# One attention-plus-gate kernel, and a new order for its opening

## The chip, the cores and the metric

The kernel runs on one core of a Trainium2 chip. The time is device microseconds of that core; lower is better. The kernel before was timed in three runs: 668.15 us in the median, 666.78 to 668.41. A further execution was profiled.

## What is computed

The inputs are q, k and v (4 batches, 8 heads, 768 positions, 64 columns each) and two weight matrices of 512 x 2048 and 2048 x 512. Cut to what matters, the reference is:

```
k_sum = max of k over blocks of 32 positions;  v_sum = mean of v over the same blocks
scores_l = q k^T / 8, kept only where |i - j| < 16;  scores_s = q k_sum^T / 8 + log(32)
a = softmax over both together
x = a [v; v_sum], heads side by side, as (3072, 512)
h = x w_in;  g = h where h >= 1, 0 where h <= -1, (h + 1)^2 / 4 between
out = g w_out
```

All inputs and outputs are float32.

## The kernel before

The 3072 rows of x are worked on in eight chunks of 384, two to a batch. For each chunk, four pairs of heads p go through attention; then 16 blocks f of the hidden width go through the two feed-forward matmuls. A float32 product is made of three matmuls in a faster 32-bit format: each operand is split into a high half (the rounded value) and a rest, and high x high, high x rest and rest x high are added. The weights have to be split once, which is part of the first chunk. They come as 16 pieces of 128 x 2 x 512 ("weight pairs", i): pair 0 holds the blocks 0 and 1 of w_in, pair i block i - 1 of w_out and block i + 1 of w_in. A piece arrives as 64-bit words, and its float32 values are put together from the two 32-bit halves of a word on the chip.

Each piece of work is a *step*, written as a letter and its indices, and these are the ones the prediction speaks of:

- `r`, `k`, `q`, `y`, `v`: loads of keys, key windows, queries, values and value windows for a chunk c and a pair of heads p; `w`: the load of a weight pair (lines 104 to 108); `m`: the load of the mask and the unit matrix.
- `K`, `R`, `C`: a window of keys is copied together, the maximum over blocks taken (line 222), and copied behind the window (225). `Y`, `Z`, `V`, `W`: the sum of values over blocks (229), its turn on TensorE (233), its mean (237), and that spread over six blocks (241).
- `S`, `M`, `E`, `D`, `N`: scores (253), mask and maximum (261, 266), exponentials (271), reciprocal of the denominator (276, 277), normalisation (281).
- `T`, `P`: turn of the probabilities on TensorE (286) and their copy out of PSUM (291 on VectorE, 293 on ScalarE). `A`, `X`, `L`: probabilities times values (300), high half of x (307 or 309) and its rest (314).
- `a`, `b`, `c`, `d`, `e`, for a weight pair: first scaling (line 118 on GpSimd, 120 on ScalarE), second scaling (125), six joins on VectorE (133, 136, 141), high half (146 on GpSimd, 148 on ScalarE) and rest (154).
- `F`: the first feed-forward matmul of chunk c, block f, quarter k (324, three matmuls); `G`, `H`, `I`, `J`, `O`: the gate (330; square at 334 on VectorE or 336 on ScalarE; 339; high half 344; rest 349); `B`: the second feed-forward matmul (358, nine matmuls); `U`, `o`: copy and store of a result.

So F030 is chunk 0, block 3, quarter 0, and c24 the fifth join of weight pair 2.

What happens in the opening (the first chunk, the preparation of all weights, the attention of the second chunk, the loads for the third) is written out by hand in the string `OPENING`: 540 steps in the order in which they enter the program. Every engine takes its own instructions from that list, strictly in that order, so a step that waits holds up everything behind it on its engine. The loads stand in SyncE's queue in the same way. Six small tables say on which engine some steps run. Behind the opening, a loop gives the order on TensorE for the remaining seven chunks; there the other engines' order is set by the scheduler.

Buffers also set the order: two for h and the gate's t, two for the gate's rests, three ("w") shared by converted weights, loaded keys and values and results, six in PSUM for everything but h.

Of the kernel before, what the change touches and what calls it, by code (L numbers as in the profile page):

```python
# [40 lines left out]
OPENING = """
r01 q01 K01 R01 C01 r00 R00 K00 C00 m S01 M01 q00 r03 S00 q03 y01 r02 R03 E010 E011 K03 C03 y00 M00 E001 w0 D01 S03
E000 N010 N011 K02 R02 a0 C02 T010 T011 Y01 Y00 P011 D00 M03 P010 b0 c00 c01 v01 Z01 V01 W01 c02 N000 N001 q02 Z00
E030 E031 c03 c04 v00 A01 V00 D03 T000 X01 P000 w1 c05 T001 P001 W00 N031 S02 T031 b1 L01 d0 N030 M02 y03 y02 v03
k10 Y03 a1 c10 c11 q10 T030 c12 c13 e0 E020 E021 D02 C10 Z03 A00 V03 P031 X00 P030 c14 w2 v02 L00 c15 W03 N021 N020
d1 S10 A03 X03 a2 F000 b2 Y02 v10 w3 T020 F010 Z02 V02 W02 w4 T021 k11 P020 P021 M10 c20 c21 E100 e1 q11 F011 F001
A02 L03 c22 X02 L02 Z10 F002 F003 a3 c23 c24 E101 D10 b3 N100 N101 a4 w5 G00 F012 V10 H00 c25 c30 c31 d2 I00 b4 T100
F013 G01 c32 c33 c34 T101 F020 F021 J00 H01 c40 c35 C11 P101 F022 P100 e2 d3 I01 J01 S11 F023 c42 c41 F030 F031 F032
c44 c43 c45 O00 G02 H02 B00 I02 b5 e3 a5 F040 O01 M11 w6 w7 d4 b6 F033 w8 w9 F041 c50 c51 J02 c52 G03 a6 c53 c54 W10
B01 F042 H03 O02 e4 I03 A10 c55 c60 F043 c61 a7 b7 J03 F050 G04 H04 B02 E110 E111 c62 c63 c64 d5 e5 F051 I04 O03 c65  # L50
c70 v11 q20 wa c71 c72 c73 c74 c75 J04 F060 a9 F052 d6 O04 e6 b9 c90 a8 c91 F061 B03 F062 c92 c93 c94 d7 F053 F063
G05 G06 k20 H05 I05 H06 B04 q13 b8 Z11 wc wb I06 c95 F070 k13 q12 wf wd v12 k12 we e7 c80 c82 c84 J05 J06 V11 F080
c81 c83 c85 F071 F081 r20 aa d9 O05 F072 Z12 F082 F073 O06 ba X10 L10 G07 H07 F083 G08 bb H08 e9 B05 I07 ac ca0 ca1
bc J07 ca2 I08 ca4 ca3 cc0 ca5 d8 D11 e8 F0a0 B06 F0a1 F090 F0a2 J08 cc1 O07 C13 O08 da F091 F0a3 F092 cc2 cc4 cc3
ea G0a ab V12 H0a cc5 cb0 I0a B07 F093 dc ad G09 H09 ec cb2 J0a B08 cb4 bd S13 F0b0 I09 F0d0 J09 cb1 cb3 cb5 F0b1
F0d1 F0b2 M13 F0d2 W12 O09 N110 C12 F0b3 cd1 cd0 cd2 be db eb O0a ae G0b H0b B09 I0b T110 cd4 cd3 ce0 ce2 J0b cd5
E130 P110 ce1 ce4 ce3 ce5 F0c0 F0d3 G0d O0b N111 B0a dd ed W11 F0c1 E131 H0d I0d D13 T111 F0c2 B0b F0c3 F0e0 P111
S12 de G0c H0c I0c bf J0c A11 X11 af ee F0e1 M12 L11 cf0 cf1 cf2 R20 E120 E121 J0d F0f0 F0e2 F0f1 N130 O0c O0d D12
cf4 cf3 cf5 B0c F0f2 F0e3 F0f3 B0d G0e H0e G0f N121 Z13 I0e H0f v13 I0f df C20 N120 T121 P121 T120 N131 F100 P120
F110 J0e V13 T131 J0f A12 T130 F111 ef O0e B0e P131 O0f W13 P130 X12 L12 A13 X13 L13 F112 F101 B0f F102 F113 F103  # L60
U01 U02 U00 o01 o02 o00
"""
# [8 lines left out]


@with_exitstack
def fused_kernel(ctx: ExitStack, tc: tile.TileContext, q2, kT, kwin, vT, vwin, w_in, w_out, mask, ident, out):
# [38 lines left out]
    def convert_top(i):  # L113


        _, top = raws[i]
        if f"{i:x}" in A_POOL:
            nc.gpsimd.tensor_scalar_mul(out=top.bitcast(F32), in0=top.bitcast(F32), scalar1=2.0 ** -112)  # L118
# [24 lines left out]
    def convert_high(i):  # L143
        halves[i] = room(i, "halves", [P, 2, 2 * DM], F32R)
        if i in HI_POOL:
            nc.gpsimd.tensor_copy(out=halves[i][:, 0], in_=converting[i].bitcast(F32))
# [141 lines left out]
    def turned(c, p, j):  # L288
        pts[c, p, j] = att.tile([P, T], F32, tag=f"pt{j}", name=f"pt{c}_{p}_{j}", bufs=1)
        if f"{c}{p}{j}" in P_DVE:  # L290
            nc.vector.tensor_copy(out=pts[c, p, j][:KA], in_=t_pss[c, p, j][:KA, :T])
# [40 lines left out]
    def gate_square(c, f):  # L332
        if f"{c}{f:x}" in H_DVE:
            nc.vector.tensor_tensor(out=ts[c, f], in0=ts[c, f], in1=ts[c, f], op=ALU.mult)  # L334
        else:
            nc.scalar.square(out=ts[c, f], in_=ts[c, f])  # L336
# [169 lines left out]
```

## Time and profile before

| | |
|---|---|
| median of 3 runs | 668.15 us |
| the profiled execution | 667.64 us, of which 665.9 us from first to last instruction (the span) |
| granted TensorE clock, mean | 0.991 |
| TensorE busy | 631.3 us (95%) |
| VectorE / ScalarE / GpSimd busy | 255.5 / 365.8 / 282.6 us |
| read from memory / written | 56.51 / 6.29 MB |

The first thing to see is that the shares of the whole span hide the opening: VectorE is busy for 38% of the span and GpSimd for 42%, but in the first fifth of it both are nearly full, and in the rest they have little to do beside a TensorE that never stops. In the profile's rows PE is TensorE, PEld its weight loads, DVE VectorE, ACT ScalarE, POOL GpSimd, SP SyncE; L118 is line 118 of the kernel; a row of a group gives the output and inputs, the shape, the count, then the busy time, the mean time of one in ns, and the idle time in front of them with the engine that ended it. A row of a timeline gives start, length, engine, line and, in brackets, the idle time ahead and what ended it.

### The profile page before, as it was taken

The page shows a single profiled execution, that of the slowest core. Times are in us where ns is not written, and L with a number is a line of the kernel's source. Part 1 is how long each engine was busy: PE and PEld are TensorE (multiplying, and loading weights), DVE is VectorE, ACT ScalarE, POOL GpSimd, SP SyncE. Part 2 cuts the span into 40 slices and gives each one's busy share as a digit, 9 for nine tenths or more (in the row PEclk, how much of TensorE's full clock was granted, in tenths as well). Part 3 has the DMA queues.
Part 4 walks back from the last instruction along what each step waited for, and adds up shares of the span by engine and source line. Part 5 has one row for each costly group of instructions (what it writes and reads, how often), then busy time and mean ns, then how long its engine had stood idle before and what let it go on. Part 6 is the DMA issues. An engine that isn't in the chain of part 4 may idle for free.

```text
span 665.9 us, 11707 instructions
## 1 busy us (share of the span) xinstructions
PE 631.3 (95%) x4448; PEld 555.1 (83%) x4448; DVE 255.5 (38%) x497; ACT 365.8 (55%) x940; POOL 282.6 (42%) x305
## 2 busy tenths in 40 slices
PE   3588899989999999999999999999999999999997
PEld 2467788768988888898888989888888998889996
DVE  5778898662222322144222422235222222211111
ACT  4678877355455554555555555465554645544332
POOL 3899997543333323333333333334323323322221
PEclk9889999999999999999999999999999999999999
DMA  9999941171113311062121401144210100000001
GB/s 308 290 320 306 313 143 53 50 252 36 53 53 105 95 53 30 25 203 91 53 53 54 143 7 50 53 151 143 53 52 22 69 19 19 1 34 14 1 1 47
DMA packets 49767, 63.55 MB, mean 95 GB/s; under 512 B 24880, under 2 KB 33328, under 8 KB 49712
## 3 DMA queue, kind: packets, MB, share of 16 engines
q1 hardware_dynamic: 49712, 62.81, 31.7%
q8 instruction: 35, 0.57, 0.4%
q14 instruction: 20, 0.16, 0.1%
HBM read 56.51 MB, written 6.29 MB: 94 GB/s over the span
## 4 chain that ended last, share of the span: by engine, by line
PE 83%; POOL 8%; DVE 3%; DMA 2%; issue 2%; ACT 1%; SPq 0%; POOLq 0%; ACTq 0%
PE acc L358 37%; PE h L324 37%; PE o_ps L300 3%; POOL halves L154 3%; POOL raw L118 3%; PE s_ps L253 3%; PE t_ps L286 3%; DMA raw<-in_w_in 1%; POOL glo L349 1%; DMA mask_sb<-in_mask 1%; POOL e L281 1%; DVE c L133 0%; DVE c L136 0%; DVE t L334 0%; PE vs_ps L233 0%
## 5 line engine op out<-in xcount | busy, mean ns | idle before, releaser
L324 PE MATMUL h<-xhi,halves 128*128 128x384 f32 x1024 | 289.9, 342 | 7.3 <-POOL halves L154 3.3
L358 PE MATMUL acc<-halves,ghi 128*128 128x512 f32 x768 | 239.6, 393 | 0.0
L349 POOL TENSOR_TENSOR glo<-t,ghi 128x384 fp32r<-128x384 f32 x128 | 129.8, 1015 | 204.4 <-ACT ghi L344 204.1
L324 PEld LDWEIGHTS h<-xhi,halves 128*128 128x128 f32 x1024 | 188.5, 189 | 18.3 <-POOL halves L154 5.8
L339 DVE SCALAR_TENSOR_TENSOR t<-h,t 128x384 f32<-128x384 f32 x128 | 71.1, 557 | 269.6 <-ACT t L336 256.1
L324 PE MATMUL h<-xlo,halves 128*128 128x384 f32 x512 | 173.1, 338 | 0.2 <-DVE xlo L314 0.2
L358 PEld LDWEIGHTS acc<-halves,ghi 128*128 128x128 f32 x768 | 144.4, 188 | 27.2
L358 PE MATMUL acc<-halves,glo 128*128 128x512 f32 x384 | 153.8, 400 | 2.6 <-POOL glo L349 2.6
L330 ACT ACTIVATE t<-h,ones_half 128x384 f32<-128x384 f32 x128 | 73.9, 578 | 125.7 <-PE h L324 120.5
L271 ACT ACTIVATE e<-e,den 128x120 f32<-128x120 f32 x192 | 73.3, 383 | 56.0 <-DVE den L266 55.9
L344 ACT CAST ghi<-t 128x384 fp32r<-128x384 f32 x128 | 65.3, 513 | 64.4 <-DVE t L339 64.4
L324 PEld LDWEIGHTS h<-xlo,halves 128*128 128x128 f32 x512 | 96.7, 189 | 4.5 <-DVE xlo L314 0.5
L358 PEld LDWEIGHTS acc<-halves,glo 128*128 128x128 f32 x384 | 72.2, 188 | 15.8 <-POOL glo L349 3.5
L281 POOL TENSOR_TENSOR e<-e,den 128x360 f32<-128x360 f32 x64 | 49.6, 796 | 54.3 <-ACT t L330 40.3
L336 ACT ACTIVATE t<-t 128x384 f32<-128x384 f32 x126 | 66.0, 525 | 3.6
L225 POOL COPY k<-ks 128x144 f32<-128x144 f32 x30 | 9.2, 308 | 70.4 <-DMA k<-in_kwin 50.9
L154 POOL TENSOR_TENSOR halves<-w,halves 128x1024 fp32r<-128x1024 f32 x16 | 38.5, 2411 | 0.9 <-ACT halves L148 0.4
L241 POOL COPY v<-v 24x640 f32<-24x640 f32 x30 | 21.5, 718 | 36.5 <-issue 32.4
L300 PEld LDWEIGHTS o_ps<-pt,v 120*64 120x64 f32 x720 | 24.7, 143 | 14.6 <-ACT ghi L344 7.4
L271 ACT ACTIVATION_READ_ACCUMULATOR e<-e,den 128x1 f32 x192 | 36.0, 187 | 0.0
L314 DVE TENSOR_TENSOR xlo<-o_ps,xhi 128x384 fp32r<-128x384 f32 x32 | 17.8, 555 | 43.1 <-ACT xhi L309 43.1
L300 PE MATMUL o_ps<-pt,v 120*64 120x64 f32 x720 | 29.1, 232 | 4.2 <-POOL v L241 2.1
(56 smaller groups left out, 437.2 us busy)
## 6 DMA issues: line engine op xcount, KB each, us to landing
k<-in_kwin SPq DMA_DIRECT2D x28, 360.0 KB, 4.2
v<-in_vwin SPq DMA_DIRECT2D x30, 288.0 KB, 3.1
raw<-in_w_in SPq DMA_DIRECT2D x16, 512.0 KB, 10.4
raw<-in_w_out SPq DMA_DIRECT2D x16, 512.0 KB, 9.9
out<-o SPq DMA_DIRECT2D x24, 256.0 KB, 2.1
q<-in_q SPq DMA_DIRECT2D x56, 96.0 KB, 4.2
kraw<-in_kT SPq DMA_DIRECT2D x13, 384.0 KB, 4.2
vraw<-in_vT SPq DMA_DIRECT2D x13, 384.0 KB, 3.7
```

The lines of the kernel that those rows point to most:

```text
L154: nc.gpsimd.tensor_tensor(out=lo, in0=converting[i].bitcast(F32), in1=hi.bitcast(F32), op=ALU.subtract)
L241: nc.gpsimd.tensor_copy(out=mean[:, 1:], in_=mean[:, :1].broadcast_to([NSUM, NB - 1, P]))
L271: nc.scalar.activation(out=e[:, t, :], in_=e[:, t, :], func=AF.Exp, bias=nm[:, t:t + 1], scale=1.0, accum_out=den[:, t:t + 1])
L281: nc.gpsimd.tensor_tensor(out=e, in0=e, in1=den.unsqueeze(2).broadcast_to([P, NT, KA]), op=ALU.mult)
L300: nc.tensor.matmul(o_pss[c, p][j * D:(j + 1) * D, cols], v_ts[c, p][:KA, blk, j * D:(j + 1) * D], pts[c, p, j][:KA, cols], start=True, sto ...
L324: nc.tensor.matmul(hs[c, f][:, :T], weight["win", f][w][:, k * P:(k + 1) * P], x, start=(k == 0 and n == 0), stop=(k == NK - 1 and n == 2))
L330: nc.scalar.activation(out=ts[c, f], in_=hs[c, f][:, :T], func=AF.Relu, bias=ones_half, scale=0.5)
L336: nc.scalar.square(out=ts[c, f], in_=ts[c, f])
L339: nc.vector.scalar_tensor_tensor(out=ts[c, f], in0=hs[c, f][:, :T], scalar=1.0, in1=ts[c, f], op0=ALU.max, op1=ALU.min)
L344: nc.scalar.copy(out=hi, in_=ts[c, f])
L349: nc.gpsimd.tensor_tensor(out=lo, in0=ts[c, f], in1=hi.bitcast(F32), op=ALU.subtract)
L358: nc.tensor.matmul(acc[c][i], a[:, rows], weight["wout", f][w], start=(f == 0 and n == 0), stop=(f == NF - 1 and n == 2))
```

## The change

The list `OPENING` holds the same 540 steps in another order, and the tables name other engines for some of them. No step is added or taken away, and nothing behind the opening changes in the source.

```diff
 OPENING = """
-r01 q01 K01 R01 C01 r00 R00 K00 C00 m S01 M01 q00 r03 S00 q03 y01 r02 R03 E010 E011 K03 C03 y00 M00 E001 w0 D01 S03
...
+r01 r00 K01 R00 R01 q01 K00 C01 C00 m q00 S01 M01 E010 E011 S00 r02 R02 M00 E000 E001 q02 r03 D01 K02 C02 K03 N010
...
-K_COPY = "gggg"
-H_DVE = "0c 0f".split()
-P_DVE = "111 121 130 131".split()
-X_DVE = "12 13".split()
-A_POOL = "0 1 2 3 4 5 9 a d".split()
-HI_POOL = [1, 5, 8, 13]
+K_COPY = "gvgg"
+H_DVE = "".split()
+P_DVE = "130".split()
+X_DVE = "".split()
+A_POOL = "".split()
+HI_POOL = [0, 1, 2, 3, 4, 5, 7, 9, 10, 11, 12, 15]
```

In words: all 16 first scalings run on ScalarE (nine ran on GpSimd). Twelve high halves of weights run on GpSimd (four did). All gate squares are on ScalarE (two were on VectorE), as are all copies of x (two were on VectorE) and all copies of turned probabilities but one (four were on VectorE). The key window of heads p = 1, the pair with which the opening starts, is copied on VectorE (all four were on GpSimd).

The first place is GpSimd's queue around the first two weight pairs. In these rows `e_...` are probabilities, `raw_...` the words of a weight pair, `w_...` its joined values, `halves_...` its two halves, `first_91` value windows, `k_0_...` a window of keys. Before:

```order
L281 TENSOR_TENSOR e_3_1_233<-e_3_1_233,den_3_235 128x360
L281 TENSOR_TENSOR e_3_0_231<-e_3_0_231,den_3_235 128x360
L118 TENSOR_SCALAR raw_293<-raw_293 128x1024
L154 TENSOR_TENSOR halves_325<-w_264,halves_325 128x1024
L225 COPY k_0_338<-ks_0_107 128x6x24
L241 COPY first_91<-first_91 24x640
L281 TENSOR_TENSOR e_2_1_330<-e_2_1_330,den_2_332 128x360
L281 TENSOR_TENSOR e_2_0_328<-e_2_0_328,den_2_332 128x360
L146 CAST halves_400<-w_389 128x1024
L118 TENSOR_SCALAR raw_391<-raw_391 128x1024
L241 COPY first_91<-first_91 24x640
L154 TENSOR_TENSOR halves_400<-w_389,halves_400 128x1024
```

And now:

```order
L281 TENSOR_TENSOR e_2_1_241<-e_2_1_241,den_2_243 128x360
L146 CAST halves_335<-w_296 128x1024
L154 TENSOR_TENSOR halves_335<-w_296,halves_335 128x1024
L281 TENSOR_TENSOR e_2_0_239<-e_2_0_239,den_2_243 128x360
L225 COPY k_0_317<-ks_0_103 128x6x24
L241 COPY first_91<-first_91 24x640
L281 TENSOR_TENSOR e_3_1_327<-e_3_1_327,den_3_329 128x360
L281 TENSOR_TENSOR e_3_0_325<-e_3_0_325,den_3_329 128x360
L146 CAST halves_476<-w_390 128x1024
L225 COPY k_1_363<-ks_1_105 128x6x24
L241 COPY first_91<-first_91 24x640
L154 TENSOR_TENSOR halves_476<-w_390,halves_476 128x1024
```

Before, the rows were the first scaling of pair 1 (raw_293), the rest of pair 0 (halves_325), the high half of pair 1 (halves_400), the first scaling of pair 2 (raw_391) and the rest of pair 1. Now the scalings are gone from the queue, and the high half of pair 0 (halves_335, which ScalarE made before) stands directly ahead of its rest.

The second place is ScalarE's queue, from the copies of the first probabilities to the first high half of x. Before:

```order
L293 COPY pt_1_1_227<-t_ps_1_1_219 120x384
L293 COPY pt_1_0_238<-t_ps_1_0_215 120x384
L125 ACTIVATE raw_183<-raw_183 128x1024
L237 ACTIVATE v_1_245<-vs_ps_1_247 24x128
L271 ACTIVATE e_3_0_231,den_3_235<-e_3_0_231,den_3_235 128x120 x3
L271 ACTIVATE e_3_1_233,den_3_235<-e_3_1_233,den_3_235 128x120 x3
L237 ACTIVATE v_0_266<-vs_ps_0_255 24x128
L309 CAST xhi_1_288<-o_ps_1_268 128x384
```

And now:

```order
L293 COPY pt_1_1_224<-t_ps_1_1_220 120x384
L293 COPY pt_1_0_237<-t_ps_1_0_212 120x384
L120 ACTIVATE raw_234<-raw_234 128x1024
L125 ACTIVATE raw_234<-raw_234 128x1024
L237 ACTIVATE v_1_248<-vs_ps_1_216 24x128
L271 ACTIVATE e_2_0_239,den_2_243<-e_2_0_239,den_2_243 128x120 x3
L271 ACTIVATE e_2_1_241,den_2_243<-e_2_1_241,den_2_243 128x120 x3
L309 CAST xhi_1_290<-o_ps_1_263 128x384
```

The first scaling of pair 0 (L120, raw_234) is new there, ahead of the second scaling (L125), of the mean of the values of heads p = 1 (L237) and of the next exponentials, which now are those of p = 2 and were those of p = 3.

On SyncE's queue the first load of keys for p = 0 (r00) now comes ahead of the queries q01, the values y00 come behind weight pair 0, and the weight pairs come in the order 0, 1, 2, 3, 5, 7, 4, 6, 8, 9, a, b, c, e, d, f. On TensorE the order of the blocks of chunk 0 is changed in the same sense (F06 begins ahead of F05, F08 ahead of F07), and in front of F000 stand T021 and Z02 where T030, T031, Z03, S10 and A03 stood before.

More of the change, by code (lines that the diff above doesn't have):

```diff
@@ L41 @@
 OPENING = """
-r01 q01 K01 R01 C01 r00 R00 K00 C00 m S01 M01 q00 r03 S00 q03 y01 r02 R03 E010 E011 K03 C03 y00 M00 E001 w0 D01 S03
[L43 to L61, printed above, removed]
+r01 r00 K01 R00 R01 q01 K00 C01 C00 m q00 S01 M01 E010 E011 S00 r02 R02 M00 E000 E001 q02 r03 D01 K02 C02 K03 N010
@@ new lines @@
+N011 y01 Y01 R03 D00 S02 T010 Z01 N000 N001 T011 P011 T000 T001 w0 P010 M02 y00 v01 v00 q03 w1 Y00 a0 b0 V01 W01 C03
+A01 Z00 c00 E020 E021 c01 c02 c03 X01 P001 V00 c04 D02 P000 S03 y02 k10 q10 v02 c05 L01 M03 W00 a1 N021 d0 e0 A00
+X00 Y02 N020 b1 w2 Z02 k11 C10 c10 L00 T021 c11 c12 E031 y03 v03 F000 T020 c13 c14 V02 P021 E030 F010 P020 D03 W02
+w3 S10 b2 a2 A02 c15 N031 N030 M10 X02 E100 F001 F011 T030 q11 Y03 Z03 V03 w5 d1 C11 W03 c20 P030 T031 P031 v10 L02
+c22 E101 w7 w4 Z10 A03 F002 X03 F012 c21 S11 b3 a3 e1 c24 D10 c23 L03 c25 N101 F013 T101 N100 G01 H01 M11 I01 c30
@@ new lines @@
+F003 d2 e2 G00 H00 I00 V10 c31 c32 c33 J01 T100 F020 F021 c34 c35 a5 F030 F022 P100 J00 F031 W10 O01 O00 F023 b5
+F032 k12 c50 B00 F033 b7 G02 c51 c52 c53 c54 c55 d3 e3 H02 B01 I02 b4 w6 a4 c40 F040 P101 A10 v11 w8 c41 c42 c43 C12
+F041 q12 d5 e5 G03 H03 J02 c44 I03 w9 F042 v12 b6 a7 O02 c45 c70 c71 F060 wa q20 r20 q13 wb F043 F061 B02 E110 J03
+G04 k20 c72 c73 k13 c74 X10 F062 H04 wc I04 c75 we a6 c60 wd c61 d4 e4 O03 c62 c63 c64 c65 J04 b8 F050 F063 F051 B03
+d7 e7 O04 G06 a9 H06 F052 Z11 Z12 I06 L10 b9 d6 V11 F053 G05 V12 H05 c90 c92 c91 I05 F080 e6 B04 F081 a8 c94 c93 W11
@@ new lines @@
+c80 J05 O05 c81 c95 c82 F070 F082 F071 F083 J06 O06 d9 e9 c83 c84 B05 F072 c85 ba aa G08 E111 D11 N111 H08 I08 S12
+bb d8 ca1 F073 M12 G07 H07 I07 J08 bc B06 F0a0 T111 ca0 ca2 ca3 ca4 ca5 F0a1 P111 J07 ab e8 C13 F090 F0a2 ae F091
+cb1 cb0 N110 O07 O08 T110 F0a3 F092 da G0a P110 H0a W12 ea cb2 cb4 cb3 B07 F093 I0a ad ac cb5 B08 F0b0 G09 db eb cc0
+cc2 cc4 S13 H09 E121 J0a bd I09 A11 M13 F0b1 cc1 cd0 cc3 cc5 be J09 F0c0 F0b2 cd2 F0c1 O09 O0a F0b3 E130 G0b H0b I0b
+cd1 dc ec E131 wf v13 cd4 E120 cd3 F0c2 B09 F0c3 J0b cd5 D12 O0b B0a F0d0 dd G0c ce0 ce2 ce4 X11 H0c Z13 L11 I0c B0b
@@ L62 @@
+af bf F0d1 ed F0e0 J0c F0d2 N121 N120 V13 W13 O0c ce1 ce3 ce5 de ee F0e1 F0d3 cf0 cf2 D13 N130 F0e2 T120 T121 F0e3
+R20 B0c P121 G0e H0e N131 cf4 I0e cf1 F0f0 P120 A12 G0d H0d I0d cf3 cf5 F0f1 J0d O0d T130 P130 F0f2 T131 F0f3 B0d
+F110 X12 J0e G0f H0f I0f J0f L12 P131 C20 df O0e ef F100 F111 A13 O0f F112 B0e X13 L13 F101 B0f U01 F102 F113 F103
+U00 U02 o00 o01 o02
 """
```

## The prediction

> **What bounds the kernel now.** I read the page's engine totals first, to see whether TensorE (PE) has any room at all, then the busy time by stretch, to see where that room lies.
>
> ```profile
> PE 631.3 (95%) x4448; PEld 555.1 (83%) x4448; DVE 255.5 (38%) x497; ACT 365.8 (55%) x940; POOL 282.6 (42%) x305
> core 0: us, PE busy (x) PEld busy (x) DVE busy (x) ACT busy (x) POOL busy (x), PEclk, DMA share, GB/s
> 0.00:34.88 34.88, 16.81 (x214) 12.69 (x214) 24.23 (x48) 18.22 (x63) 22.51 (x40) 0.92 0.99 296
> 34.88:133.14 98.26, 88.74 (x589) 74.33 (x588) 80.09 (x140) 70.73 (x143) 86.11 (x59) 0.98 0.68 197
> 133.14:665.90 532.76, 525.72 (x3649) 468.12 (x3648) 151.17 (x310) 276.81 (x734) 174.03 (x207) 1.00 0.21 64
> 20.00:110.00 90.00, 76.35 (x534) 64.11 (x538) 76.45 (x137) 69.10 (x149) 87.84 (x62) 0.94 0.85 244
> ```
>
> TensorE is busy 525.7 of the last 532.8 us, and none of that is touched: the change orders the opening only. The opening runs from 0 to the end of step F103, and TensorE is idle there for 18.1 us before the first feed-forward matmul (F000) and for 98.26 - 88.74 = 9.5 us after it. From 20 to 110 us GpSimd (POOL) works 87.8 of 90 us, while VectorE (DVE) works 76 and ScalarE (ACT) 69. So in the opening GpSimd sets the pace. The timeline gives the marks, and the waits of that stretch say on whom TensorE waits:
>
> ```profile
> 34.88 0.69 PE L324 MATMUL h<-xhi,halves 128*128 128x384 f32 x1
> 51.35 0.44 PE L324 MATMUL h<-xhi,halves 128*128 128x384 f32 x1 [0.27 <-POOL halves L154]
> 132.87 0.34 PE L324 MATMUL h<-xhi,halves 128*128 128x384 f32 x1
> PE h L324 <- POOL halves L154: 3.3, 4, 1.3
> PE t_ps L286 <- POOL e L281: 2.4, 1, 2.4
> PE acc L358 <- POOL glo L349: 1.9, 2, 1.7
> 34.88:51.35 16.47, 12.98 (x101) 10.65 (x99) 12.66 (x25) 13.13 (x31) 16.32 (x11) 0.86 1.07 333
> 51.35:133.14 81.79, 75.75 (x489) 63.68 (x490) 67.43 (x116) 57.59 (x113) 69.79 (x49) 1.00 0.60 169
> ```
>
> The rows are F000, F030 (the first matmul that needs weight pair 2) and the end of F103, 132.87 + 0.34 = 133.2 us. Of TensorE's 9.5 us of idle time, 3.3 + 2.4 + 1.9 = 7.6 end on a GpSimd result. The length of the opening is therefore (start of F000) + (matmul work behind it) + (idle), and the change acts on all three.
>
> **The change, part by part.** Prices come from the groups by line and shape, 0 to 133 us:
>
> ```profile
> L118 POOL TENSOR_SCALAR raw<-raw 128x1024 f32<-128x1024 f32 x9 | 26.4, 2938 | 2.1 <-DMA raw<-in_w_in 2.1
> L146 POOL CAST halves<-w 128x1024 fp32r<-128x1024 f32 x4 | 4.2, 1047 | 0.6 <-DVE w L141 0.6
> L154 POOL TENSOR_TENSOR halves<-w,halves 128x1024 fp32r<-128x1024 f32 x16 | 38.5, 2411 | 0.9 <-ACT halves L148 0.4
> L120 ACT ACTIVATE raw<-raw 128x1024 f32<-128x1024 f32 x7 | 8.1, 1154 | 0.0
> L148 ACT CAST halves<-w 128x1024 fp32r<-128x1024 f32 x12 | 12.5, 1043 | 4.9 <-DVE w L141 4.9
> L336 ACT ACTIVATE t<-t 128x384 f32<-128x384 f32 x14 | 7.3, 526 | 0.2
> L293 ACT COPY pt<-t_ps 120x384 f32<-120x384 f32 x12 | 5.5, 481 | 1.6 <-PE t_ps L286 0.9 <-PE o_ps L300 0.5
> L334 DVE TENSOR_TENSOR t<-t 128x384 f32<-128x384 f32 x2 | 2.9, 1432 | 0.9 <-ACT t L330 0.9
> L291 DVE COPY pt<-t_ps 120x384 f32<-120x384 f32 x4 | 2.2, 546 | 1.6 <-PE o_ps L300 1.6
> L281 POOL TENSOR_TENSOR e<-e,den 128x360 f32<-128x360 f32 x16 | 12.7, 813 | 2.7 <-DVE den L277 2.6
> L241 POOL COPY v<-v 24x640 f32<-24x640 f32 x6 | 4.3, 718 | 0.4
> L225 POOL COPY k<-ks 128x144 f32<-128x144 f32 x7 | 2.2, 313 | 0.2
> ```
>
> Nine first scalings leave GpSimd, 9 x 2.94 = 26.4 us, and cost ScalarE 9 x 1.15 = 10.4. Twelve high halves instead of four run on GpSimd: 8 x 1.05 = 8.4 us more there, 8 x 1.04 = 8.3 less on ScalarE. Two gate squares (line 334) take 2.9 us off VectorE and put 2 x 0.53 = 1.1 on ScalarE. Three copies of turned probabilities and two of x take 5 x 0.55 = 2.7 off VectorE and put 5 x 0.48 = 2.4 on ScalarE (the copies of x have the same 384 columns, so I use one price). One key window, three copies with 560 columns in all, goes from GpSimd to VectorE, which has no such copy in this trace. Its nearest row is line 291, 0.55 us for 384 columns; scaled to 560 that is 0.8, and with two more starts I take 1.0, bounds 0.5 and 2.0, and as much off GpSimd. It ends before the query load that the first scores wait for. In sum over the opening: GpSimd 108.6 (22.51 + 86.11) - 26.4 + 8.4 - 1.0 = 89.6 us, VectorE 104.3 (24.23 + 80.09) - 2.9 - 2.7 + 1.0 = 99.7, ScalarE 89.0 (18.22 + 70.73) + 10.4 - 8.3 + 1.1 + 2.4 = 94.6. GpSimd goes from the fullest engine to the emptiest.
>
> By the Trainium skill's page GPSIMD Engine Reference, section Engine selection, an operation with one input runs at about line rate on GpSimd. By it, a scaling of 1024 columns should cost there what the 1024-column cast costs, 1.05 us; nine moved ones would free 9.4 us, not 26.4, GpSimd would keep all but 2.0 of its 108.6 us, and with the idle time behind F000 as it was the kernel would gain only 6.4 - 2.2 = 4.2 us by the terms below and take 664. The cast agrees with the rule (1047 ns), line 118 does not (2938 ns, nine of nine), so here the row decides and the rule gets no chance of its own.
>
> *First term, the start of F000.* It hangs on weight pair 0:
>
> ```profile
> 18.01 1.10 ACT L125 ACTIVATE raw<-raw 128x1024 int32<-128x1024 uint32 x1 [1.12 <-DMA raw<-in_w_in]
> 18.09 2.86 POOL L118 TENSOR_SCALAR raw<-raw 128x1024 f32<-128x1024 f32 x1 [2.15 <-DMA raw<-in_w_in]
> 20.98 1.29 DVE L133 TENSOR_SCALAR c<-raw 128x512 int32<-128x512 int32 x2 [2.96 <-POOL raw L118]
> 24.55 0.65 DVE L141 CUSTOM_DVE_ANT_0 w<-raw,c 128x1024 uint16<-128x1024 uint16 x1
> 29.21 2.38 POOL L154 TENSOR_TENSOR halves<-w,halves 128x1024 fp32r<-128x1024 f32 x1
> 16.03 0.86 ACT L293 COPY pt<-t_ps 120x384 f32<-120x384 f32 x2 [0.56 <-PE t_ps L286]
> ```
>
> The load landed just before 18.0. In the new order one 384-KB load (y00) fewer stands ahead of it, 1.3 us at the 296 GB/s of the first stretch: 16.7. ScalarE is free at 16.9 (end of the two copies), which I put 0.5 later because q01 now comes behind r00: 17.4. The scaling ends at 17.4 + 1.15 = 18.5; six joins took 20.98 to 25.20 = 4.2 us, and they now meet a denominator step that waits for six exponentials, which I put at 0.4: 23.1. GpSimd first does a spread and a normalisation (to 25.0), then the high half, 1.05, and the rest, 2.41: F000 at 28.5, that is 6.4 us earlier. Bounds: 26.7 if GpSimd is free at 23.2; 31.6 (29.21 + 2.38) if nothing of the pair comes sooner.
>
> *Second term, work moved.* Behind F000 now stand T030, T031, S10 and A03; ahead of it T021 (Z03 and Z02 change places too, and cancel). By these rows (two turns, 24 scores, 24 value matmuls):
>
> ```profile
> 120.78 0.82 PE L286 MATMUL t_ps<-ident_sb,e 128*120 128x128 f32 x6
> 109.75 0.85 PE L253 MATMUL s_ps<-k,q 64*64 64x120 f32 x24
> 110.52 0.92 PE L300 MATMUL o_ps<-pt,v 120*64 120x64 f32 x24
> ```
>
> 0.82 + 0.85 + 0.92 - 0.41 = 2.2 us: the work behind F000 becomes 88.7 + 2.2 = 90.9.
>
> *Third term, idle time behind F000.* From pair 0's rest to pair 2's rest GpSimd now has to do five normalisations (line 281), two copies of key sums (225), two spreads (241), two highs and two rests: 4.1 + 0.6 + 1.4 + 2.1 + 4.8 = 13.0, so 41.5; one spread (W03) waits about 1.8 for ScalarE, which comes to its source only behind exponentials of chunk 1: 43.3. TensorE has 12.98 us of work there, plus 1.3 of the moved 2.2: 28.5 + 14.3 = 42.8. So F030 waits 0.5, at 43.3, against 51.35. From there to F103 TensorE needs 75.75 + 0.9 us. GpSimd has 89.6 in all, of which what it did until then is 25 (the sum of its queue to pair 2's rest by these prices): 64 left, so the engine that was the bound has 12 us of room. Before, TensorE idled 6.0 us in that stretch (81.79 - 75.75). I take 4, not 0, since all four engines are still 75 to 85% full and wait on each other in order. Idle: 0.5 + 4 = 4.5 against 9.5, bounds 0 and 9.5.
>
> Sum: F103 ends at 28.5 + 90.9 + 4.5 = 123.9, 9.3 us sooner. The rest stays: 665.9 - 9.3 = 656.6 of span, 1.7 more as before (667.64 - 665.9) = 658.3, and the median of the three runs is 0.5 over the profiled run: **659 us**. The corners: F000 at 31.6 with 9.5 idle gains 1.1 (667); F000 at 26.7 with no idle gains 15.5 (652.6).
>
> **Rivals.** *ScalarE becomes the bound and the change is slower.* It carries the most added work, and each scaling now stands in its queue with the exponentials, gate activations and copies behind it. These rows span its queue from pair 0 to the last gate copy:
>
> ```profile
> 18.01:123.35 105.34, 89.09 (x633) 74.42 (x633) 89.08 (x158) 80.96 (x177) 98.69 (x70) 0.95 0.78 222
> 122.84 0.51 ACT L344 CAST ghi<-t 128x384 fp32r<-128x384 f32 x1
> L125 ACT ACTIVATE raw<-raw 128x1024 int32<-128x1024 uint32 x16 | 18.5, 1154 | 1.1 <-DMA raw<-in_w_in 1.1
> ```
>
> It idles 24.4 us in 105.3. With 5.6 us more work and the same idle time its last gate copy comes at 17.4 + 80.96 + 5.6 + 24.4 = 128.4; GpSimd's rest (1.0), the last nine output matmuls (2.1), three groups of line 324 (1.6) and hand-overs (0.2) end F103 at 133.3: no gain, 668. It decides from 24 us of idle time on. The scalings wait for loads now, where the rows show 1.1 us of such waits on ScalarE and 2.1 on GpSimd; 3 us more of it gives 671. Against it: part of that idle time was waiting for matmuls and for GpSimd's rests, which come sooner now; my sum leaves it 123.9 - 4.9 - 17.4 - 86.6 = 15 us of idle time, and that is enough only if those waits shrink.
>
> *The lead is given back at the loads.* The DMA engines are full to 51 us (shares of 0.99 and 1.07 in the stretches above) and busy until the last weight:
>
> ```profile
> 78.62 0.42 SPq L105 DMA_DIRECT2D raw<-in_w_in  x1
> raw<-in_w_in SPq DMA_DIRECT2D x16, 512.0 KB, 10.4
> ```
>
> The last weight was issued at 78.6 and landed near 89; the bytes ahead of it are the same, so TensorE, 8 us ahead at F030, comes closer to the loads. Two scalings, joins, high and rest take about 10 us: 99, and only the last output steps, 6 us of matmuls, need it, so the last pair is covered by 18 us. The middle ones are not: pairs 4, 6 and 8 to 11 would be scaled on ScalarE within 3 us of landing. If each of five pairs costs 1 us of TensorE, 5 of the 9.3 go: 664.
>
> *TensorE never waits behind F000*: 4.5 more, 654.5.
>
> **How the numbers follow.** 659 with its own spread of 656 to 662.5 has 0.56; the loads take part of the lead (662.5 to 666), 0.17; no waiting or an earlier F000 (below 656), 0.13; ScalarE's queue, 0.14, half of it within 2 us of before and half slower. About 0.3% (2 us) is what a measurement can tell from no change. Faster 0.86, same 0.07, slower 0.07. The range for 8 in 10 is 654.5 to 667.
>
> **What would show it.** F000 near 28.5 and F030 near 43; line 118 gone; 20 to 110 us with GpSimd below 80 of 90 and ScalarE the one that rises; the stretch behind F103 again 532.7. Wrong if F000 starts after 31.6, if TensorE's idle time behind it is over 9.5, or if ScalarE idles over 24 us before its last gate copy.

## The result

| | median | range | runs |
|---|---|---|---|
| before | 668.14 us | 666.78 to 669.46 | 7 |
| after | 663.65 us | 662.60 to 665.50 | 7 |

The ratio of the means is 0.9942, with a 95% interval of 0.9925 to 0.9959: faster. The median is 4.5 us lower. The forecast was 659 us, 9.1 less than before. The direction was right; half of the gain is missing. Ratios here and below are of means; they, and the median of e12, leave out one slow execution of e12 (1038.02 us, at a granted clock of 0.57).

### The profile page after: what moved, and what is told of

The parts are those of the page before. It is cut to its first block, busy times and chain, and to the rows that moved or that the text cites. A ratio compares the mean times of both kernels' runs of the same rounds, so it can differ in the third digit from the quotient of the medians.

```text
span 661.8 us, 11703 instructions
## 1 busy us (share of the span) xinstructions
PE 631.8 (95%) x4448; PEld 557.3 (84%) x4448; DVE 254.9 (39%) x494; ACT 370.3 (56%) x948; POOL 263.6 (40%) x300
## 4 chain that ended last, share of the span: by engine, by line
PE 84%; DMA 9%; DVE 4%; ACT 1%; SPq 1%; issue 1%; POOL 0%; DVEq 0%; ACTq 0%
PE h L324 37%; PE acc L358 37%; PE o_ps L300 3%; DMA raw<-in_w_in 3%; PE s_ps L253 3%; PE t_ps L286 3%; DMA first<-in_vwin 2%; DMA q<-in_q 2%; DMA v<-in_vwin 1%; DMA first<-in_kT 1%; DVE w L141 1%; DVE c L133 1%; DVE c L136 1%; SPq L108 0%; DVE t L339 0%
## 5 line engine op out<-in xcount | busy, mean ns | idle before, releaser
L261 DVE SCALAR_TENSOR_TENSOR e<-s_ps,mask_sb 128x360 f32<-128x360 f32 x64 | 30.9, 523 | 7.1 <-PE s_ps L253 6.8
```

The costliest lines, as they stand in the source:

```text
L261: nc.vector.scalar_tensor_tensor(out=es[c, p, j], in0=s_pss[c, p][j][:, :NT * KA].rearrange("p (t n) -> p t n", n=KA), scalar=1.0 / math.s ...
```

## The profile after

First the busy time by stretch, cut at F000 (28.76), shortly before F030 (47.90) and shortly before the end of F103 (128.95), and over the same 20 to 110 us as before:

```profile
core 0: us, PE busy (x) PEld busy (x) DVE busy (x) ACT busy (x) POOL busy (x), PEclk, DMA share, GB/s
28.76:47.90 19.14, 15.29 (x145) 12.69 (x143) 15.76 (x31) 13.86 (x39) 12.48 (x14) 0.82 1.08 309
47.90:128.95 81.05, 76.02 (x497) 65.06 (x495) 66.97 (x112) 63.31 (x124) 64.21 (x51) 1.00 0.65 188
128.95:661.80 532.85, 526.66 (x3649) 469.06 (x3648) 152.27 (x310) 276.78 (x734) 173.64 (x207) 1.00 0.21 63
20.00:110.00 90.00, 79.88 (x591) 67.96 (x592) 81.31 (x143) 76.61 (x170) 73.48 (x62) 0.96 0.88 254
```

From 20 to 110 us GpSimd works 73.5 us instead of 87.8, ScalarE 76.6 instead of 69.1. The stretch behind F103 lasts 532.85 us (532.76 before). So all of the gain lies in the opening, and GpSimd is relieved as foreseen. TensorE (PE) idles 8.9 us between F000 and F103 (3.85 + 5.03), nearly as long as before (9.5). The timeline shows where, in the first of the two stretches:

```profile
28.76 0.67 PE L324 MATMUL h<-xhi,halves 128*128 128x384 f32 x1
37.02 0.28 PE L233 MATMUL vs_ps<-ident_sb,vs 128*24 128x128 f32 x1 [2.43 <-DVE vs L229]
38.53 1.92 PE L300 MATMUL o_ps<-pt,first 120*64 120x64 f32 x24 [0.80 <-ACT pt L293]
46.84 0.45 PE L324 MATMUL h<-xhi,halves 128*128 128x384 f32 x1 [0.63 <-DVE t L339]
36.01 0.95 DVE L229 TENSOR_REDUCE vs<-first 128x24 f32<-128x768 f32 x1 [1.87 <-DMA first<-in_vT]
34.08 1.12 ACT L125 ACTIVATE raw<-raw 128x1024 int32<-128x1024 uint32 x1 [2.58 <-DMA raw<-in_w_in]
```

TensorE no longer waits for GpSimd there but for VectorE and ScalarE, and these wait for loads: VectorE until 36.01 for the values y03, ScalarE until 34.08 for weight pair 2, with the copies P030 and P031 behind it in its queue, which the value matmuls at 38.53 need. The waits over 28 to 129 us say the same. These are the rows that end on a DMA; in the answer for before, from 28 to 133 us, there is none:

```profile
ACT raw L125 <- DMA raw<-in_w_in: 3.8, 3, 2.6
DVE vs L229 <- DMA first<-in_vT: 2.5, 2, 1.9
ACT raw L120 <- DMA raw<-in_w_in: 1.3, 1, 1.3
POOL k L225 <- DMA k<-in_kwin: 0.6, 1, 0.6
```

## Experiments: the two halves of the change

The first pair asks whether the engine tables give the gain, or the order.

**e1_old_engines**: the kernel after with the tables of before.

```diff
-K_COPY = "gvgg"
-A_POOL = "".split()
-HI_POOL = [0, 1, 2, 3, 4, 5, 7, 9, 10, 11, 12, 15]
...
+K_COPY = "gggg"
+A_POOL = "0 1 2 3 4 5 9 a d".split()
+HI_POOL = [1, 5, 8, 13]
```

> The new order of the opening with the six tables of before: nine first scalings are back on GpSimd, eight of the high halves back on ScalarE. Theory 1 (the relief of GpSimd pays): its queue is 108.6 us long again, now in an order made for 89.6, and F000 waits for a 2.9 us scaling; F103 ends at 133 or later, time 668 to 674. Theory 2 (the order of the steps and loads pays, the engines do not): F103 near 129, time 663 to 665.

Measured: 677.13 us, 1.0141 [1.0124, 1.0158]. TensorE waits for GpSimd again, and longer than before the change:

```profile
30.60 0.69 PE L324 MATMUL h<-xhi,halves 128*128 128x384 f32 x1 [1.43 <-POOL halves L154]
46.21 0.70 PE L286 MATMUL t_ps<-ident_sb,e 128*120 128x128 f32 x3 [2.95 <-POOL e L281]
71.95 0.44 PE L324 MATMUL h<-xhi,halves 128*128 128x384 f32 x1 [2.83 <-POOL halves L154]
```

**e2_new_engines**: the kernel before with the tables of after.

```diff
-K_COPY = "gggg"
-A_POOL = "0 1 2 3 4 5 9 a d".split()
-HI_POOL = [1, 5, 8, 13]
...
+K_COPY = "gvgg"
+A_POOL = "".split()
+HI_POOL = [0, 1, 2, 3, 4, 5, 7, 9, 10, 11, 12, 15]
```

> The order of before with the six tables of the change. Theory 1: GpSimd has 19 us less, pair 0 is scaled in 1.15 instead of 2.9 us, VectorE no longer waits 9.6 us for line 118; F103 ends 2 to 5 us before 133.2, time 663 to 666. Theory 2: the engines alone bring nothing, 667 to 670.

Measured: 671.98 us, 1.006 [1.0043, 1.0076], which no theory had. TensorE waits 3.25 us at 85.02 for a rest of weights, and GpSimd had stood 4.85 us ahead of that rest, waiting for a high half from ScalarE: the old order does not fit the new engines. The order alone costs 9.5 us (677.13 less 667.6, its before), the tables alone 4.4, both together gain 4.5. So with the new order the relief of GpSimd is needed, as the first theory says, but in the old order it brings no gain.

## Experiments: where the lead went

**e3_y03_first**: one load moved up.

```diff
-... S03 y02 k10 q10 v02 ... E031 y03 v03 F000 ...
+... S03 y02 y03 k10 q10 v02 ... E031 v03 F000 ...
```

> The changed kernel with one load moved: the values of heads 3 (y03) ahead of the key window and queries of chunk 1 (k10, q10). Theory L (the lead of 6 us at F000 is given back at the loads of weight pair 2 and of y03, because the DMA engines are full): y03 lands some 4 us sooner, weight pair 2 about 1.3 later, k10 and q10 1.3 later; the 2.4 us wait of TensorE for the sum of those values goes, but pair 2 still holds F030: gain 0 to 1.5 us, 662 to 664. Theory S (the added work and waits in ScalarE's queue hold TensorE there): no change, 663.5 to 664.

Measured: 663.69 us, 0.9937 [0.9923, 0.9951], as the kernel after. VectorE's wait is gone, and TensorE waits for ScalarE in its place, which waits for pair 2:

```profile
34.71 0.28 PE L233 MATMUL vs_ps<-ident_sb,vs 128*24 128x128 f32 x1 [0.45 <-DVE vs L229]
38.49 0.75 PE L300 MATMUL o_ps<-pt,first 120*64 120x64 f32 x4 [3.07 <-ACT pt L293]
```

**e4_more_load** and **e5_more_load_before**: 0.75 MB more to load, ahead of pair 2, in the kernel after and in the kernel before.

```diff
 def fetch(i):
+    if i == 2:
+        for n, spare in enumerate(spares):
+            nc.sync.dma_start(out=spare, in_=kT[1, n][:, :512])
```

> The changed kernel with three loads of 256 KB more, into room that nothing else uses, just ahead of weight pair 2. At 309 GB/s they take 2.5 us of the DMA engines. Theory L: weight pair 2 and y03 land 2.5 us later, F030 starts 2 to 2.5 us later, and most of it stays in the total: 665 to 666.5. Theory S: the loads have slack there, at most 0.5 us in the total: 663.5 to 664.2.

> The kernel before with the same three loads of 256 KB (2.5 us of transfer in all, into room that holds nothing) ahead of weight pair 2. Added to the kernel after, they cost 1.9 us. Theory L (the change took the slack out of the loads: after it the opening waits for data, before it for GpSimd): here they cost at most 0.7 us, so 667.5 to 668.3, and PE's waits ahead of F103 still end with GpSimd. Theory B (2.5 us more of transfer cost nearly that in any kernel that moves so much in its opening): 669.3 to 670.5.

Measured: after plus loads 665.59 us, 0.9964 [0.9952, 0.9976], 1.9 over the kernel after; before plus loads 669.95 us, 1.0029 [1.0019, 1.0040], 2.2 over its own before. So neither has 2.5 us of slack in its loads. The second is a miss for the theory that the kernel before has plenty; it was taken up again below, the other way round.

**e6_reordered**: loads and steps of the first 45 us in another order.

```diff
-... S03 y02 k10 q10 v02 ... b1 w2 Z02 k11 C10 ... y03 v03 F000 ... w3 S10 b2 a2 ... M10 X02 E100 ... V03 ... P030 T031 P031 ...
+... S03 y02 v02 y03 w2 v03 k10 q10 ... b1 Z02 w3 k11 ... F000 ... X02 b2 T030 Z03 V03 a2 ... P030 T031 P031 ... C10 ... S10 ... E100 ...
```

> The kernel after, with the same table of engines, and the order of its opening changed between S03 and k12: the loads of y02, v02, y03, weight pairs 2 and 3 and v03 go ahead of k10, q10, k11, q11; the scores, masks, exponentials and norms of the first head of chunk 1 move some 20 steps down; the copies P030 and P031 and the spread V03 come between or ahead of ScalarE's two operations on pair 2. Theory L (the 4.4 us lost between F000 and F030 are lost because ScalarE stands at the load of pair 2 with V03, P030 and P031 behind it, and VectorE at y03): F030 begins at 43 to 45 instead of 47.97, PE idles under 2 us between F000 and F030 instead of 3.85, the end falls to 659 to 661.5. Theory C (PE has only so much work of which the operands are there; what is not lost ahead of F030 is lost at the copies of pairs 3 to 5 behind it): F030 earlier, but F103's end within 1 us of 128.95 and the time within 663 to 664.5.

Measured: 663.89 us, 0.9938 [0.9923, 0.9953]. The first theory's 659 to 661.5 fell. The profiled execution was the shortest of six (661.51): there TensorE idled 3.3 us between F000 and F020 in waits of this order's own (1.44 for a copy, 1.82 for a gate), and F020 began at 42.29. A profile of one execution is not the median.

**e7_tail**: the end of the list changed, to do away with a wait of 2.40 us behind F103 that both kernels have.

```diff
-... F101 B0f U01 F102 F113 F103 U00 U02 o00 o01 o02
+... F101 F102 F103 G10 H10 I10 F113 J10 G11 H11 I11 J11 B0f U01 U00 U02 o00 o01 o02
```

> The kernel after with the last entries of the order changed alone: the gates G10 to J11 are written out between F103 and B0f, and B0f and U00 to U02 come behind them. PE's wait of 2.40 us at 132.24 (for the first gate product behind the opening, which is in both kernels) should go if ScalarE's and VectorE's steps of B0f and U00 to U02 stood ahead of those gates: 661.0 to 662.3. If the gates are late for another reason (the results of F103 themselves): 663 to 664.5.

Measured: 664.51 us, 0.9955 [0.9939, 0.9971]. The wait went and another came, 10 us later:

```profile
141.89 0.27 PE L233 MATMUL vs_ps<-ident_sb,vs 128*24 128x128 f32 x1 [3.50 <-DVE vs L229]
```

Its opening is that of the kernel after, so it is also a second look at that one. F020 began at 44.92, 1.9 us sooner than in the kernel after, and yet it is no earlier behind 66 us. The granted clock was full from F000 to there, where the kernel after has a mean of 0.91:

```profile
28.54:67.00 38.46, 33.89 (x257) 28.26 (x257) 34.18 (x61) 31.14 (x69) 31.43 (x28) 1.00 1.08 295
```

So what is won ahead of F030, in waits or in clock, does not set the end here.

**e9_pair2_behind**: y03 as in e3, and `b2 a2` moved behind P031 in ScalarE's queue. The joins of pair 2 stay where they were, so the first of them, c20, works on words that are not scaled yet: its result is not the reference's, but its work is the same in kind and size.

```diff
-... S03 y02 k10 ... S10 b2 a2 A02 ... c20 P030 T031 P031 ...
+... S03 y02 y03 k10 ... S10 A02 ... c20 P030 T031 P031 b2 a2 ...
```

> The kernel after with y03 loaded ahead of k10, and ScalarE's two operations on weight pair 2 (b2, a2) moved from ahead of A02 to behind P031; nothing else. With y03 alone moved, the time did not change (663.7) and A03 still began at 38.49 behind copies that stood behind b2 and a2. Theory L: A03 now begins at 36 to 37, PE's idle time between F000 and F030 falls to about 1 us; pair 2's halves come 1.5 to 2 us later on GpSimd, which F020 (46.84) would feel, so the gain is 0 to 1.5 us: 662 to 663.7. Theory S (ScalarE's sum of work bounds this stretch, whatever its order): A03 early, but the rest as late as before or later: 663.5 to 665.

Measured: 663.92 us, 0.9946 [0.993, 0.9963]. The value matmuls begin at 37.05 instead of 38.53, and at 41.35 the scores wait 2.13 us for the queries of the next chunk. Again a wait only changed its place.

Set side by side, the traces show one thing that stays: ScalarE's first scaling of weight pair 9 (`a9`) waits for its load in every kernel with the order of after, at nearly the same moment, and the scores of chunk 2 (S20, behind F103) begin a fixed time behind it (the 1.6 us more in two rows are a fall of the clock, shown in the last section).

| kernel | a9 begins | waited for its load | S20 begins | between |
|---|---|---|---|---|
| after | 66.55 | 1.27 | 129.00 | 62.45 |
| e9 | 66.94 | 2.04 | 129.37 | 62.43 |
| e7 | 67.00 | 2.32 | 131.00 | 64.00 |
| e3 | 67.53 | 2.24 | 131.57 | 64.04 |
| e4 (more loads) | 68.29 | 1.92 | 130.72 | 62.43 |

How the wait reaches TensorE stands in four rows of the kernel after: the scaling, the gate (its square stands behind a9 on ScalarE), the next feed-forward matmul, and the rest on GpSimd:

```profile
66.55 1.16 ACT L120 ACTIVATE raw<-raw 128x1024 f32<-128x1024 f32 x1 [1.27 <-DMA raw<-in_w_in]
68.21 0.56 DVE L339 SCALAR_TENSOR_TENSOR t<-h,t 128x384 f32<-128x384 f32 x1 [0.99 <-ACT t L336]
68.91 0.41 PE L324 MATMUL h<-xhi,halves 128*128 128x384 f32 x1 [0.45 <-DVE t L339]
70.15 2.41 POOL L154 TENSOR_TENSOR halves<-w,halves 128x1024 fp32r<-128x1024 f32 x1 [1.48 <-ACT halves L148]
```

In the kernel after itself this costs TensorE little, 0.45 us here and 0.35 at 72.61. It shows in e7, which is 1.9 us ahead at F020: its scaling of pair 9 waits 2.32 us and begins no sooner. The moment is not the same in every execution: in the profiled one of e6, the shortest of its six, pair 9 has the same loads ahead of it and is scaled at 64.91 without a wait.

## Experiments: pair 9, or the amount of data

**e13_pair9_up**: one entry moved.

```diff
-... b4 w6 a4 ... A10 v11 w8 ... F041 q12 ... I03 w9 F042 ...
+... b4 w6 w9 a4 ... A10 v11 w8 ... F041 q12 ... I03 F042 ...
```

> The kernel after with one entry moved: the load of weight pair 9 stands right behind that of pair 6, ahead of v11, pair 8 and q12 (1.4 MB, some 4.5 us of transfer) instead of behind them. In all runs with the order of after, ScalarE's scaling of pair 9 waits for that load and begins at 66.55 (after), 66.94, 67.00, 67.53, and at 68.29 with 2.5 us of extra loads, whatever was lost or won ahead of it, and S20 begins 62.4 us later (64.0 where the clock dips at 116). Theory P (the landing of pair 9, which ScalarE waits for with its gates behind, sets the pace of the opening): the wait goes, the scaling begins at 64.5 to 65.5, S20 at 127 to 128, the time falls by 1 to 2 us to 661.6 to 662.7. Theory F (the loss ahead of F030 sets the end, pair 9's wait costs nothing): 663.3 to 664.2.

Measured: 664.38 us, 0.9935 [0.9916, 0.9954]: no gain. Now pair 8 comes late, at the same moment:

```profile
66.51 1.19 ACT L125 ACTIVATE raw<-raw 128x1024 int32<-128x1024 uint32 x1 [3.08 <-DMA raw<-in_w_in]
```

Two pairs must have come by then, in whichever order, so it is not the place of pair 9.

**e10_weights_first** and **e11_reordered_weights_first**: all weight pairs ahead of the keys and queries of the last two heads of chunk 1, in the order of after and in that of e6.

```diff
-... F032 k12 ... w6 ... A10 v11 w8 ... C12 F041 q12 ... w9 F042 v12 ... F060 wa q20 r20 q13 wb ... k20 ... k13 ... wc ... we ... wd ... wf v13 ...
+... F032 w6 ... b4 w8 w9 ... A10 v11 wa ... F041 wb ... I03 v12 ... F042 wc k12 q12 ... F060 we wd wf F061 k13 q13 ... c84 C12 ... q20 k20 r20 v13 ...
```

> The kernel after with all weight pairs from 6 on loaded ahead of the keys and queries of the last two heads of chunk 1 (k12, q12, k13, q13), the values v11 and v12 between them, and the loads for chunk 2 (q20, k20, r20) behind the last pair; C12 moves down with k12. Theory P: no wait for a pair behind 60 us; with the wait of 1.06 us for pair c at 82.5 gone too, 660.5 to 662.5. Theory F: 663 to 664.2. If the keys of chunk 1 now come late for S12 (92.5): 664 to 666.

> The order of e6_reordered (what F030 waits for loaded and done first) and the loads of e10_weights_first together. Theory P: both waits that set the pace one after the other (pair 2 at 34, pair 9 at 66.5) are gone, and the time falls to 658.5 to 661. Theory F: as e6_reordered, 663 to 664.2.

Measured: 668.78 us, 1.0001 [0.9988, 1.0015], and 665.32 us, 0.9967 [0.9946, 0.9987]. No pair is waited for behind 60 us, but in e10 the keys k12 come at 88, with GpSimd's whole queue behind the copy that needs them, and TensorE 4.5 us behind GpSimd:

```profile
88.48 0.30 POOL L225 COPY k<-ks 128x144 f32<-128x144 f32 x1 [6.82 <-DMA k<-in_kwin]
89.58 0.68 PE L286 MATMUL t_ps<-ident_sb,e 128*120 128x128 f32 x2 [4.52 <-POOL e L281]
```

**e12_late_third**: only the loads for chunk 2 moved back.

```diff
-... F060 wa q20 r20 q13 wb ... G04 k20 ... E131 wf v13 ...
+... F060 wa q13 wb ... G04 ... E131 wf q20 k20 r20 v13 ...
```

> The kernel after with only the loads for chunk 2 (q20, k20, r20, 0.84 MB, 2.8 us) moved from ahead of pairs b and c to behind pair f. They stand behind pair 9. Theory P: ScalarE's wait of 1.06 us for pair c at 82.5 goes or shrinks, the one for pair 9 stays at 66.5 to 67; S20 falls by 0 to 1 us: 662.6 to 663.8. If the pace is set by all loads up to the last (theory B, 1 us of load is nearly 1 us of time wherever it stands): 661 to 662.

Measured: 665.14 us, 0.995 [0.993, 0.9969], not told apart from the kernel after. The wait for pair c went; a9 still began at 67.50 and S20 62.45 us later. What is loaded behind pair 9 does not set the pace.

By then seven edits had moved loads and gained nothing, so the next four took data away. In **e14_less_load**, **e15_less_load_before**, **e16_one_mb_less** (pairs 4 and 5 alone) and **e17_less_load_reordered** the second half of some weight pairs is not loaded; a constant stands for these weights, so their results are not the reference's, and every later step is the same.

```diff
+for n, i in enumerate([2, 3, 4, 5, 6, 7, 8]):
+    early[i] = room(i, "raw", [P, 2, DM, 2], I32)
+    eng = nc.vector if n % 2 else nc.gpsimd
+    eng.memset(early[i][:, 1].rearrange("p n w -> p (n w)").bitcast(F32), 1.125)
 do(OPENING)
```

> The kernel after, in which the second half of each of the weight pairs 2 to 8 (7 x 512 KB, 3.5 MB, some 11.5 us of transfer at 305 GB/s) is not loaded; it holds a constant that VectorE and GpSimd write in the first 4 us, while they wait for data. All other work is the same, with that constant for these weights. Theory D (the amount of data that must have come sets the pace of the kernel after): no wait for a load behind 40 us, S20 at 123 to 126.5 instead of 129.0, the time 658 to 661. Theory W (the engines' work sets it, the waits for loads are hidden or would come back elsewhere): 662.5 to 664.

> The kernel before with the same 3.5 MB not loaded. Theory D, in which the kernel before waits for GpSimd and not for loads (no wait for a load from 28 to 110 us in its trace): 666 to 668, less than 2 us gained. If 2.5 us of extra loads, which cost it 2.2 us, say that loads set its pace as well: 658 to 663.

> The kernel after with the second halves of pairs 4 and 5 alone not loaded (1 MB, 3.4 us). Theory D: the scaling of pair 9 no longer waits and begins at 64.3 to 65.5 instead of 66.55, S20 at 126.8 to 128, the time 661.3 to 662.6. Theory W: 663.3 to 664.3.

> The order of e6_reordered with the same 3.5 MB not loaded. Theory D: what PE waits for between F000 and F030 is gone as well: S20 at 121 to 125, the time 656 to 660, below e14_less_load by 0.5 to 2 us. Theory W: 662.5 to 664.

Measured: the kernel after with 3.5 MB less 658.96 us, 0.9867 [0.9855, 0.988]; the kernel before with 3.5 MB less 667.75 us, 0.9999 [0.9989, 1.0008]; the kernel after with 1 MB less 662.79 us, 0.992 [0.9903, 0.9936]; the order of e6 with 3.5 MB less 663.03 us, 0.9933 [0.9922, 0.9945]. Of the kernel after with 3.5 MB less, the scaling of pair 9, S20 and the stretch between F000 and S20:

```profile
61.29 1.14 ACT L122 ACTIVATE raw<-raw 128x1024 f32<-128x1024 f32 x1
123.70 0.84 PE L255 MATMUL s_ps<-k,q 64*64 64x120 f32 x24
```

```profile
28.06:123.70 95.64, 89.64 (x639) 76.44 (x639) 81.98 (x141) 77.13 (x163) 77.12 (x64) 1.00 0.64 184
```

And the same stretch of the kernel after:

```profile
28.76:129.00 100.24, 91.36 (x640) 77.75 (x638) 82.73 (x142) 77.16 (x162) 76.69 (x64) 0.97 0.73 211
```

It is 4.6 us shorter in e14: 2.9 us less idle time of TensorE and 1.7 less matmul time, at a clock of 1.00 instead of 0.97. That the clock alone is not the cause, e7 showed; the constants are not either, since e15 has them and gains nothing.

This decides between the two theories. The same 3.5 MB are worth 4.7 us to the kernel after and nothing to the kernel before, which still waits for GpSimd. In e14 no engine waits for a load from 28 to 110 us, pair 9 is scaled 5.3 us sooner, and S20 begins 62.41 us after that, the same time as behind a scaling that waited: behind pair 9 the work takes equally long, and the moment at which pair 9 is scaled decides. With 1 MB less the scaling begins at 64.94 and S20 at 127.31, the dose in between. The order of e6 does not gain from it: it is held by waits of its own, as above, and the 656 to 660 expected of it were wrong. The interval of the run with 1 MB less overlaps that of the kernel after, so its gain shows in the trace and not in the time.

**e18_keys_behind_pair9**: what is not needed yet goes behind pair 9, and GpSimd's steps on it move down with it.

```diff
-... F032 k12 ... b4 w6 a4 ... A10 v11 w8 ... C12 F041 q12 ... I03 w9 F042 v12 ... F060 wa q20 r20 q13 wb F043 ... k20 ... k13 ... wc ... we ... wd ... V11 ... e8 C13 ... wf v13 ...
+... b4 w6 w8 w9 a4 ... I03 k12 F042 wa wb ... F060 q12 v11 v12 F043 wc we k13 q13 wd wf ... V11 C12 ... cb5 C13 ... q20 k20 r20 v13 ...
```

> The kernel after with the loads of k12, v11, q12 (0.74 MB, 2.4 us) moved from ahead of pair 9 to behind it, the loads of chunk 2 behind pair f, k13 and q13 between pairs e and d, and GpSimd's steps C12 and C13 moved down to where these keys have come. Theory D: pair 9's scaling no longer waits (64.3 to 65.5), S20 at 127 to 128, 661.5 to 662.8; if k12 or k13 come late again, as the keys did with all weights first (PE waited 4.52 us at 89.58): 664 to 668.

Measured: 660.25 us, 0.9903 [0.9888, 0.9918], 3.4 us under the kernel after, and its interval does not touch that one's. It is also below the 661.5 to 662.8 expected; k12, v11 and q12 are 0.86 MB by the sizes in the DMA rows (360, 288 and 192 KB), 2.8 us at 305 GB/s, and why the gain is larger is not shown. All data are loaded and all steps done, so it is the version to keep. Its scaling of pair 9, S20 and the copy of the key sums of k12 on GpSimd:

```profile
62.53 1.18 ACT L120 ACTIVATE raw<-raw 128x1024 f32<-128x1024 f32 x1
125.01 0.85 PE L253 MATMUL s_ps<-k,q 64*64 64x120 f32 x24
65.91 0.32 POOL L225 COPY k<-ks 128x144 f32<-128x144 f32 x1
```

Pair 9 is scaled without a wait, S20 comes 62.48 us later, and the copy at 65.91 waits for nothing, unlike in e10. Some of the lead in this trace is chance: pair 2, which is loaded in the same place as in the kernel after, was taken up at 31.71 instead of 34.08.

**e19_half_queries**: the first queries in two pieces, only the half that is read.

```diff
-nc.sync.dma_start(out=q_t, in_=blocks)
+for rows in halves_of:
+    nc.sync.dma_start(out=q_t[rows, :, rows], in_=blocks[rows, :, rows])
```

> The kernel after with the first chunk's queries loaded in two pieces each, only the half that is read (4 x 192 KB less, 0.77 MB), in rows of 256 bytes instead of 512. Theory D by bytes: 2.5 us less to load ahead of all, the landing of pair 9 at 64, S20 at 127 to 128, 661 to 662.5. If the time of a load goes by its rows and not by its bytes: no change, 663.2 to 664.4, or later if the four more loads are issued late at the start.

Measured: 666.20 us, 0.9979 [0.9969, 0.9989]; 2.5 us slower than the kernel after with 768 KB less to load. To 28 us the transfers run at 258 GB/s (305 in the kernel after to 28.76), at the same share of the DMA engines (0.96 and 0.97):

```profile
0.00:28.00 28.00, 12.59 (x158) 9.81 (x158) 18.55 (x41) 14.85 (x49) 11.38 (x29) 1.00 0.96 258
```

Here the load of shorter rows was not cheaper for having fewer bytes. The Trainium skill's page DMA: Bandwidth & Descriptors, section Specifications, gives 512 bytes as the least for line rate; rows of 256 bytes instead of 512 bear that out here in direction.

## Why the prediction was right or wrong

*What bounds the kernel before:* right that it is not the loads, since without 3.5 MB of them it takes the same 667.75 us. That it is GpSimd alone is not shown: its waits say so, and with its old work the new order takes 677, but relieved within the old order (e2) the kernel became 4.4 us slower.

*First term, the start of F000:* 28.5 predicted, 28.76 measured; pair 0 was scaled at 17.36 (17.4). The single copies of the key window on VectorE took 0.6 us where 1.0 was taken.

*Second term, the moved work:* 90.9 us predicted, 91.3 measured (15.29 + 76.02), with 0.82 of the clock in the first stretch; at a full clock (e14) it is 89.6, so the agreement holds for that clock only.

*Third term, the idle time behind F000:* this is the step that failed. "So F030 waits 0.5, at 43.3": it began at 47.97, 19.2 us behind F000 instead of 14.8, of which 15.3 were matmul work (14.3 predicted) and 3.9 idle time (0.5 predicted). From there on the sum was right, 80.65 us predicted, 81.0 measured. The idle time was 8.9 us, not 4.5, which is the missing 4.5 of gain. The step followed GpSimd's queue and TensorE's work to F030, and took the loads of pair 2 and y03 as there, though its own rows had the DMA engines full in that stretch (1.07). But the loss between F000 and F030 is not the cause by itself: e7 was 1.9 us ahead at F020 and then waited for pair 9 until 67.0. What the step put at nothing is the waits for loads, at pair 2 and y03 first and at pairs 8 and 9 behind them, and with 3.5 MB less to load the missing 4.7 us are there. The new order adds to these waits itself: in the list of before, v11, q12 and k12 stand behind pair 9, in the new one ahead of it, and e18, which moves them back, gained 3.4 us. The prediction compared only the bytes ahead of the last weight.

*The sum without loads* came out: 123.9 for the end of F103, 659 us in all. The kernel after with 3.5 MB less begins S20 at 123.70 and takes 658.96. That is luck in part, since its terms cancel there: F030 at about 44.4 (43.3 predicted) and 1.3 us less from F030 on, or 89.6 us of matmul work (90.9) and 6.0 of idle time (4.5).

*The rivals.* "The lead is given back at the loads", 664 us, was the right one in kind; that its time came out is luck, for it was a guess. Of the pairs that it named, 8 or 9 is the one that is waited for, and pair 2, which it left out, is waited for longest. It was given 0.17. Its sign stood in the rows: DMA shares near 1 up to the last weight. I read there that the last pair is covered by 18 us, and gave the middle ones a guess of 1 us each. The loads up to and with pair 9, 19.0 MB by the sizes in the DMA rows, take 64 us at the 296 GB/s of the prediction's first row, and e14, in which nothing waits for a load, scales pair 9 at 61.29: a sum of bytes would have shown that the work comes too early there. In the kernel after, at 305 GB/s, as many bytes had been moved by 62 us, and pair 9 was taken up 4 us later; those 4 us are not explained. ScalarE's queue as the bound did not come: from 20 to 110 us it works 76.6 of 90 us, and it waits for loads rather than holding them. The 664 us that the prediction works out for a scaling of 1.05 us on GpSimd is near the time measured, but not for that reason: GpSimd was busy for 89.9 us up to 128.95, as the rows had it (89.6).

*The signs named:* F000 near 28.5, GpSimd below 80 of 90, ScalarE as the one that rises and 532.7 us behind F103 all came true; F030 near 43 did not, and showed the miss. VectorE rose too, from 76.5 to 81.3. None of the three signs of being wrong came, so they were set too wide: F000 began before 31.6, the idle time behind it was 8.9 and not over 9.5, and ScalarE idled 18 us before its last gate copy, not over 24.

*Still open:* why the kernel before, which does not gain from fewer loads, loses as much as 2.2 us from more. A part stands in the trace of e5, where ScalarE waits for pair 2; without the extra loads it took that pair up at 35.37, and waited for nothing:

```profile
35.95 1.15 ACT L128 ACTIVATE raw<-raw 128x1024 int32<-128x1024 uint32 x1 [1.05 <-DMA raw<-in_w_in]
```

So pair 2 comes just ahead of need in the kernel before. In that trace S20 begins 0.7 us later (133.85 instead of 133.14); the rest of the 2.2 us is not shown. And e6's order lost in the median what its profiled execution had won; why was not tried.

## What to carry to other kernels

When an engine is relieved, sum up next what must have been loaded by each mark and divide by the rate of the transfers: a queue that is full from the start is a clock of its own. Here no other order of the work beat it, only another order of the loads in it. To tell a true bound from a wait that merely shows, take the suspected resource's load away instead of moving it: seven edits that moved loads gained nothing, one that left out 3.5 MB showed 4.7 us in one kernel and none in the other, and after it the move that pays was found (e18). A load that is moved back must take the steps that need it along, or it holds up a whole in-order queue.
